# Replacing an implicit instruction schedule by one that is planned forward and backward: a bucketed attention, gated MLP and MLP kernel on one core

## The chip, the core and the metric

The kernel runs on one core of a Trainium2 chip. The core has five engines with a queue of instructions each: PE (matrix products and transposes), DVE (vector work), ACT (activations; it also issues some DMAs), POOL (elementwise work on GpSimd) and SP (it only issues DMAs here). Every engine takes its own queue strictly in order and waits where an operand isn't ready or a buffer isn't free. The metric is the time of one execution on the device in microseconds (us); of several executions the median is given.

## The reference

Three stages follow each other; B=2, H=8, S=768, D=64, model width 512. The reference in numpy, cut to what is computed:

```python
# attention: a key counts for a query only if both hash to the same bucket
q_bits = (einsum('bhsd,dk->bhsk', q, proj) > 0)        # 6 bits, likewise k_bits
mask = q_bucket[:, :, :, None] == k_bucket[:, :, None, :]
scores = where(mask, matmul(q, k.T) / sqrt(D), -1e9)
x = matmul(softmax(scores), v)                         # heads joined: (2, 768, 512)
# gated MLP with a product over the sequence
h = maximum(x @ w_in, 0); u, vh = h[..., :512], h[..., 512:]
v_n = (vh - mean(vh)) / sqrt(var(vh) + 1e-6)
v_s = einsum('ts,bsd->btd', w_spatial, v_n) + b_spatial[None, :, None]
y = (u * v_s) @ w_out
# second MLP with layernorm and residual
yn = (y - mean(y)) / sqrt(var(y) + 1e-6) * g_ln
return y + maximum(yn @ w_ch1, 0) @ w_ch2              # w_ch1 512x2048, w_ch2 2048x512
```

## The kernel before

Products are made in three passes of a 32-bit format: each operand is split into a high part (a rounded copy, on ACT or POOL) and a low part (the difference, on POOL or DVE), and high by high, high by low and low by high are added up. The three weights w_in, w_out and w1/w2 arrive as 64-bit floats. Each is taken in pieces of 512 columns (`stage_f64` loads one on ACT's queue into a tile `f64_...`, here written f_w, f_u, ...), turned into two 32-bit words on ACT and DVE (L102 to L107, tile f64c_...), added on POOL (L111) and split. w_out, w_v and w_u are converted during the attention, stored in device memory (`kept`) and loaded again for the second batch (`reload`, L515). The pieces of w1 and w2 are converted beside the second part and stay in SBUF.

Attention goes over 48 groups of two q tiles of 128 rows (batch, head, g). For one group PE makes the scores sc (L308, eight matmuls into the one PSUM buffer of that tag), DVE takes the maximum and clips (L319, tile x), ACT the exponential (L332), PE transposes x (pt, L346), ACT and DVE copy it to e, and PE multiplies with v (po, L360); ACT and DVE put the result into xT. Per pair of heads `pair_load` fetches k and q, `mismatch` makes the bucket signs (pm, m), `pair_split` the high and low parts (on POOL), and `passes_of` copies them by DMAs on SP's queue into ks and qs, from which sc is made. At the end of a pair `normalized` makes pz on PE and multiplies xT by it.

`moe1(b)` is the gated MLP of one batch, a generator that is advanced between other work: for six row tiles t, act_x (xT split), pv for the v half and later the u half, the statistics; then pg (product with w_spatial, pieces w_sp on SP's queue), gt (bias and gate, DVE L618), ptr_g (its transposes), act_g (its parts), py (product with w_out), y, and a store to y_dram. The first batch runs beside the attention of the second one. The second MLP works on three chunks c of 512 rows: layernorm of rows from y_dram (`ln_stats`: statistics bst_c, mv, scaling of xc; `ln_x`: px_c on PE, xh on ACT and DVE), then for each of 16 slices f `up` (pc, 12 matmuls, then ch on ACT and DVE) and `down` (12 matmuls into four tiles acc). Runs of (c, f) are c=0 and c=1 with f<5 first, then c=2 whole, then the rest of c=1 and c=0.

What sets the order before: the program is written in stages that are advanced by hand (`attn_step`, tables such as CONV_AT, `fill`), and Tile's own list scheduler, with a simulated time line (`schedule_with_timeline_sim=True`), reorders it. Parts of it are pinned: `tc.issue_after(...)` holds conversions, pair stages and w_sp loads behind the last maximum or exponential (CPIN, `last["late"]`), `mm3_after` chains the projections of batch 1, `high_priority` favours `moe1(1)`. The resulting order of every engine is fixed when the kernel is built.

Of the kernel before, what the change touches and what calls it, by code (L numbers as in the profile page):

```python
# [8 lines left out]
F32 = mybir.dt.float32  # L9
# [18 lines left out]

@with_exitstack
def attn_moe_kernel(ctx: ExitStack, tc: tile.TileContext, qT, kT, v, proj, w_in, w_spT, b_sp, w_out, g_ln, w1, w2, out):  # L30
    nc = tc.nc
# [20 lines left out]
    CPIN = ("max", "exp")  # L52
# [5 lines left out]
    PIN = (1,)  # L58
    HP = 0
# [197 lines left out]
    last = {}  # L257
# [55 lines left out]
    def masked_max(b, h, g, j):  # L313
# [5 lines left out]
        last["max"] = nc.vector.tensor_scalar(  # L319
# [121 lines left out]
    def mm3(ps, pairs):  # L441

        n, tot = 0, len(pairs) * 3
        for lh, rh in pairs:
            for i, j in PASSES:
                mm = nc.tensor.matmul(ps, lh(i), rh(j), start=(n == 0), stop=(n == tot - 1)).ins  # L446
                n += 1
        return mm

    def mm3_free(key, *args):  # L450
        mm3(*args)

    def mm3_after(key, *args):

        if key in last:
            with tc.issue_after(last[key]):
                last[key] = mm3(*args)
        else:
            last[key] = mm3(*args)
# [57 lines left out]
    def moe1(b, ps_m, tag):  # L517
# [19 lines left out]
        def v_half(t):  # L537
# [10 lines left out]
            last["moe"] = st_last[0]  # L548
# [57 lines left out]
        for t in range(NQT + 1):  # L606
            if t < NQT:
# [276 lines left out]
```

## Time and profile before

| | us |
|---|---|
| timed executions | 735.76, 735.81, 737.73 (median 735.81) |
| the profiled execution: its time | 737.73 |
| its span, first to last instruction | 737.7 |
| PE busy | 681.1 |
| DVE, ACT, POOL busy | 429.7, 310.8, 192.1 |
| mean granted PE clock | 0.971 of full |

The span starts with the first instruction and ends with the last; all positions below, such as 340–362, are us from its start. The attention of batch 0 runs to about 186; that of batch 1, with the gated MLP of batch 0 beside it, to about 350; the gated MLP of batch 1 with the first slices of the second MLP to about 475; the rest of the second MLP to the end.

### The profile page before, as it was taken

The numbers are of one execution on the slowest core, as the hardware profiler recorded it, in microseconds if no ns is written. First come the engines' busy times: TensorE is split into PE (matmuls) and PEld (weight loads), VectorE is DVE, ScalarE is ACT, GpSimd is POOL, SyncE is SP. The second block draws the span as 40 slices with busy tenths as digits, with TensorE's granted clock in tenths as the row PEclk, the third lists the DMA queues.
The fourth block names the chain that finished last, engine by engine and source line by source line (L and its number), as shares of the span: only waits on it lengthen the run. The fifth ranks groups of instructions, "written<-read, shape, count | busy, mean of one in ns | idle before, by whom it ended". The sixth has DMA issues, their size and how long they took to land.

```text
span 737.7 us, 10036 instructions
## 1 busy us (share of the span) xinstructions
PE 681.1 (92%) x3644; PEld 528.0 (72%) x3644; DVE 429.7 (58%) x818; ACT 310.8 (42%) x607; POOL 192.1 (26%) x189
## 2 busy tenths in 40 slices
PE   6998999895999999998899997799988899999997
PEld 5765667664777767776688886587766688888885
DVE  3586797784765645444898458676899812112112
ACT  2685878683565645444373231443232310100100
POOL 2224333315242222010143233234454500000000
PEclk8899999998999999999899998989999999999999
DMA  7664787575473563212533242533223101001001
GB/s 185 177 159 109 192 252 192 163 199 133 112 242 89 177 194 85 80 51 78 200 115 143 71 149 92 187 116 114 86 86 115 57 1 58 0 1 57 1 1 57
DMA packets 51514, 84.36 MB, mean 114 GB/s; under 512 B 6382, under 2 KB 35798, under 8 KB 50442
## 3 DMA queue, kind: packets, MB, share of 16 engines
q1 hardware_dynamic: 38426, 54.37, 26.1%
q10 hardware_dynamic: 13040, 29.36, 12.3%
q8 instruction: 29, 0.48, 0.3%
q14 instruction: 19, 0.16, 0.1%
HBM read 51.12 MB, written 12.58 MB: 86 GB/s over the span
## 4 chain that ended last, share of the span: by engine, by line
PE 60%; DMA 12%; DVE 12%; issue 5%; ACT 5%; POOL 4%; SPq 1%; ACTq 0%; DVEq 0%; POOLq 0%
PE acc L756 12%; PE pc L446 11%; PE pv L446 8%; PE sc L308 8%; PE po L360 6%; PE pg L616 5%; PE pt L346 5%; DMA f_w<-in_w 5%; PE py L446 3%; POOL f64c_w L111 2%; DMA wst_sp<-in_w_spT 2%; DVE f_w L105 2%; DVE x L319 1%; DMA f_u<-in_w_in 1%; ACT x L332 1%
## 5 line engine op out<-in xcount | busy, mean ns | idle before, releaser
L756 PE MATMUL acc<-w2t,ch 128*128 128x512 f32 x576 | 146.0, 396 | 7.7 <-DVE ch L747 6.3
L446 PE MATMUL pc<-xh,w1t 128*128 128x512 f32 x576 | 146.2, 399 | 2.7 <-DVE xh L740 2.7
L756 PEld LDWEIGHTS acc<-w2t,ch 128*128 128x128 f32 x576 | 106.9, 188 | 36.7 <-DVE ch L747 10.8
L446 PEld LDWEIGHTS pc<-xh,w1t 128*128 128x128 f32 x576 | 109.8, 191 | 28.5 <-ACT f64c_w L102 2.9
L319 DVE TENSOR_SCALAR_CACHE_REDUCE x<-sc 128x768 f32<-128x768 f32 x96 | 89.7, 951 | 32.3 <-PE sc L308 30.0
L308 PE MATMUL sc<-ks,qs 128*128 128x512 f32 (+3 forms) x384 | 86.4, 364 | 17.5 <-DMA ks<-k 8.3
L332 ACT ACTIVATE x<-x,nb 128x768 f32<-128x768 f32 x96 | 89.4, 933 | 26.3 <-DVE x L319 24.5
L747 DVE SCALAR_TENSOR_TENSOR ch<-pc,ch 128x512 fp32r<-128x512 f32 x48 | 33.0, 687 | 109.4 <-ACT ch L746 109.4
L346 PE MATMUL pt<-ident,x 128*128 128x128 f32 x576 | 81.2, 280 | 5.3 <-ACT x L332 3.0
L346 PEld LDWEIGHTS pt<-ident,x 128*128 128x128 f32 x576 | 67.9, 144 | 23.7 <-ACT x L332 9.5
L308 PEld LDWEIGHTS sc<-ks,qs 128*128 128x128 f32 (+1 forms) x384 | 59.2, 199 | 32.0 <-issue 21.1
L746 ACT ACTIVATE ch<-pc 128x512 fp32r<-128x512 f32 x48 | 28.4, 592 | 127.3 <-PE pc L446 127.3
L360 PE MATMUL po<-e,vv 128*64 128x256 f32 x576 | 75.0, 397 | 5.0 <-DVE m L247 1.9
L349 ACT ACTIVATE e<-pt 128x384 f32<-128x384 f32 x120 | 55.5, 487 | 34.5 <-PE pt L346 31.8
L111 POOL TENSOR_TENSOR f64c_w<-f_w,f64c_w 128x512 f32<-128x512 f32 x32 | 43.6, 1362 | 97.0 <-DVE f64c_w L107 82.9
L360 PEld LDWEIGHTS po<-e,vv 128*64 128x64 f32 x576 | 37.8, 139 | 29.8 <-issue 7.1
L351 DVE COPY e<-pt 128x384 f32<-128x384 f32 x72 | 39.6, 550 | 20.0 <-PE pt L346 19.7
L616 PE MATMUL pg<-vn,w_sp 128*128 128x512 f32 x180 | 46.8, 413 | 0.0
L102 ACT ACTIVATE f64c_w<-f_w 128x512 f32<-128x512 f32 x32 | 21.4, 670 | 58.3 <-DMA f_w<-in_w 51.1
L616 PEld LDWEIGHTS pg<-vn,w_sp 128*128 128x128 f32 x180 | 34.9, 198 | 8.0
L446 PE MATMUL pv<-w_u,act_x 128*128 128x512 f32 x144 | 37.9, 410 | 2.7 <-DMA w_u<-ws_u 2.7
L446 PE MATMUL py<-w_out,act_g 128*128 128x512 f32 x144 | 36.3, 396 | 2.1 <-ACT act_g L435 2.1
(133 smaller groups left out, 804.7 us busy)
## 6 DMA issues: line engine op xcount, KB each, us to landing
f_w<-in_w ACTq DMA_DIRECT2D x32, 512.0 KB
ks<-k SPq DMA_DIRECT2D x48, 192.0 KB
qs<-q SPq DMA_DIRECT2D x48, 128.0 KB
wst_sp<-in_w_spT SPq DMA_DIRECT2D x12, 384.0 KB
w_out<-ws_out SPq DMA_DIRECT2D x2, 2048.0 KB
vv<-in_v SPq DMA_DIRECT2D x16, 192.0 KB
qs<-q SPq DMA_DIRECT2D x48, 64.0 KB
ot<-y_dram SPq DMA_DIRECT2D x12, 256.0 KB
```

The source lines that it names most:

```text
L111: nc.gpsimd.tensor_tensor(cf, tf, cf, op=ALU.add)
L308: nc.tensor.matmul(sc[:, csl], qs[:rows, i, qsl], ks[:rows, i, csl], start=(i == 0), stop=(i == 1))
L319: last["max"] = nc.vector.tensor_scalar(x, t["sc"], MASKED, FMAX, op0=ALU.min, op1=ALU.min, accum_out=nb,).ins
L332: last["exp"] = nc.scalar.activation(t["x"], t["x"], AF.Exp, bias=t["nb"], scale=-1.0, accum_out=z_sum[b][:, n, h : h + 1]).ins
L346: nc.tensor.transpose(pt[:, i, :], t["x"][:, kt * P : (kt + 1) * P], ident)
L349: nc.scalar.activation(e, pt, AF.Copy)
L351: nc.vector.tensor_copy(e, pt)
L360: nc.tensor.matmul(po[a : a + D, :GW], heads[b, h]["vv"][:, kt], gr["e"][:, kt], start=(kt < 2), stop=(kt >= NKT - 2))
L446: mm = nc.tensor.matmul(ps, lh(i), rh(j), start=(n == 0), stop=(n == tot - 1)).ins
L616: nc.tensor.matmul(pg, w[i][:, k], vn[:, j, k, :], start=(n == 0), stop=(n == len(order3) - 1))
L747: last["lo"] = nc.vector.scalar_tensor_tensor(ch[:, 1], pc, 0.0, ch[:, 0].bitcast(F32), op0=ALU.max, op1=ALU.subtract).ins
L756: last["mm"] = nc.tensor.matmul(accs[c][t], ch[:, i, t * P : (t + 1) * P], w2t[f][:, j, 0, :], start=(start and n == 0), stop=(stop and n ...
```

## The change

The body of the kernel is hardly touched: the same calls `nc.tensor...`, `nc.vector...` are made in the same sequence, but `nc` is now a recorder (`Plan`). Tiles are placeholders (`Later`, `View`) and pools only notes (`Pool`, `Ring`). Every call becomes a `Job` with its engine, a cost from a small table (`cost`) and the jobs it must wait for; up to six matmuls of one shape into one tile are one job. `gates` adds the waits for free buffers. `run` goes forward through the jobs with one clock per engine: whichever engine can start first takes, of its jobs that are ready, the one with the smallest rank (by position in the program at first, later by the latest time at which it may start). Work of the other engines is opened only when PE has come within 60 jobs of it (LOOK) and not earlier than 20 us before it is due (EARLY). `latest` goes backward from the end and gives each job that due time. `settle` repeats the two twelve times and keeps the round with the earliest end. `issue` then emits all jobs by (part, start) under Tile's manual scheduling, so nothing reorders them any more. There are three parts: 0 is attention with `moe1(0)`, 1 `moe1(1)` with the first slices of the second MLP, 2 the rest; every engine finishes a part before it begins the next. All `issue_after`, `high_priority` and `mm3_after` are gone, and xc has eight buffers instead of six. No operation is added to or taken from the computation. In the trace of the changed kernel all instructions carry the line of `issue` (L476).

```diff
+    RUN = 6
+    LOOK = 60
+    EARLY = 20.0
+    ROUNDS = 12
...
+    def settle(self):
+        best = None
+        late = None
+        for n in range(self.ROUNDS):
+            end = self.run(late)
+            if best is None or end < best[0]:
+                best = (end, {j: (j.start, j.end) for j in self.jobs})
+            late = self.latest()
...
+            t, e, c = best
+            j = min((j for j in c if ready[j] <= t + 1e-9), key=rank)
...
+    def issue(self):
+        self.gates()
+        self.settle()
+        order = sorted((j for j in self.jobs if j.engine), key=lambda j: (j.part, j.start, j.at))
...
+        with self.tc.manual_schedule():
+            for j in order:
...
-    nc = tc.nc
+    fixed = ctx.enter_context(tc.tile_pool(name="fixed", bufs=1))
+    ident = fixed.tile([P, P], F32, name="ident")
+    make_identity(tc.nc, ident)
+    nc = plan = Plan(tc)
...
         for e in pair_steps.get(i, ()):
-            with tc.issue_after(last["exp"]):
-                e()
+            e()
...
-        xc = m2a.tile([P, DM], F32, tag="xc", name=f"xc_{c}_{len(xcs.setdefault(c, []))}", bufs=TPC + 2)
+        xc = m2a.tile([P, DM], F32, tag="xc", name=f"xc_{c}_{len(xcs.setdefault(c, []))}", bufs=TPC + 4)
...
+    plan.issue()
```

Three places of the new order. In the rows a name is followed by its batch, head or tile numbers and a running number; then come shape and count.

First, POOL at the start of batch 1 (k2_1_1 and q2_1_1 are the heads 2 and 3 of batch 1, act_x0 the parts of xT for `moe1(0)`; a TENSOR_SCALAR row is a high part, the 128x384 rows k's low part). Before:

```order
L228 TENSOR_SCALAR k2_1_1_1850<-k2_1_1_1850 128x768
L228 TENSOR_SCALAR q2_1_2_2293<-q2_1_2_2293 128x768
L86 TENSOR_TENSOR act_x0_0_2190<-xT_0_186,act_x0_0_2190 128x512
L86 TENSOR_TENSOR act_x0_1_2193<-xT_0_186,act_x0_1_2193 128x512
L86 TENSOR_TENSOR act_x0_2_2243<-xT_0_186,act_x0_2_2243 128x512
L86 TENSOR_TENSOR k2_1_1_1850<-k2_1_1_1850 128x384 x2
L111 TENSOR_TENSOR f64c_u_1_1816<-f64_u_1_1786,f64c_u_1_1816 128x512
L86 TENSOR_TENSOR w_u_0_1753<-f64c_u_1_1816,w_u_0_1753 128x512
```

and in the changed kernel:

```order
L476 TENSOR_SCALAR q2_1_1_1809<-q2_1_1_1809 128x768
L476 TENSOR_SCALAR k2_1_1_1816<-k2_1_1_1816 128x768
L476 TENSOR_TENSOR f64c_u_1_1811<-f64_u_1_1739,f64c_u_1_1811 128x512
L476 TENSOR_TENSOR k2_1_1_1816<-k2_1_1_1816 128x384 x2
L476 TENSOR_TENSOR w_u_0_1746<-f64c_u_1_1811,w_u_0_1746 128x512
L476 TENSOR_TENSOR act_x0_0_2071<-xT_0_347,act_x0_0_2071 128x512
L476 TENSOR_TENSOR act_x0_1_2121<-xT_0_347,act_x0_1_2121 128x512
L476 TENSOR_TENSOR act_x0_2_2133<-xT_0_347,act_x0_2_2133 128x512
```

The low part of k2_1_1 has moved from behind the three act_x0 to in front of them, and the high part of q2_1_2 no longer stands between k's high and low part.

Second, `moe1(1)` at its fifth row tile. On PE before, from the product pg_1_4 to the transposes ptr_g1_4 that need gt_1_4:

```order
L616 MATMUL pg_1_4_4583<-vn_1_3814,w_sp1_4_1_4478 128x512 x6
L616 MATMUL pg_1_4_4583<-vn_1_3814,w_sp1_4_0_4477 128x512 x11
L446 MATMUL py_1_3_4632<-w_out_1_4175,act_g1_3_4574 128x512
L616 MATMUL pg_1_4_4583<-vn_1_3814,w_sp1_4_0_4477 128x512
L446 MATMUL py_1_3_4632<-w_out_1_4175,act_g1_3_4574 128x512 x9
L446 MATMUL pc_0_4_4677<-xh_0_3964,w1t_4_4454 128x512
L446 MATMUL py_1_3_4632<-w_out_1_4175,act_g1_3_4574 128x512
L446 MATMUL pc_0_4_4677<-xh_0_3964,w1t_4_4454 128x512
L446 MATMUL py_1_3_4632<-w_out_1_4175,act_g1_3_4574 128x512
L433 MATMUL ptr_g1_4_4648<-ident_58,gt_1_4_4602 128x128 x4
L616 MATMUL pg_1_5_4656<-vn_1_3814,w_sp1_5_1_4580 128x512 x6
```

and in the changed kernel:

```order
L476 MATMUL pg_1_4_4550<-vn_1_3969,w_sp1_4_1_4493 128x512 x6
L476 MATMUL pg_1_4_4550<-vn_1_3969,w_sp1_4_0_4435 128x512 x12
L476 MATMUL acc_0_0_0_4283<-w2t_2_4447,ch_0_2_4405 128x512 x3
L476 MATMUL acc_0_0_1_4289<-w2t_2_4447,ch_0_2_4405 128x512 x3
L476 MATMUL acc_0_0_2_4296<-w2t_2_4447,ch_0_2_4405 128x512 x3
L476 MATMUL acc_0_0_3_4302<-w2t_2_4447,ch_0_2_4405 128x512 x3
L476 MATMUL py_1_3_4616<-w_out_1_4141,act_g1_3_4545 128x512 x12
L476 MATMUL ptr_g1_4_4634<-ident_58,gt_1_4_4593 128x128 x4
L476 MATMUL pc_0_4_4642<-xh_0_4023,w1t_4_4527 128x512 x6
```

Between the end of pg_1_4 and ptr_g1_4 there now stand the twelve acc matmuls and the whole of py_1_3. On DVE, which makes gt_1_4, the rows in front of it were

```order
L167 BN_AGGR mv_1_4531<-bst_c1_1_4539 128x2
L105 SCALAR_TENSOR_TENSOR f64_w1_5_4894<-f64_w1_5_4894,f64c_w1_5_4896 128x512
L83 TENSOR_TENSOR w_sp1_5_1_4580<-wst_sp1_5_4577,w_sp1_5_0_4579 128x768
L167 BN_AGGR mv_1_4531<-bst_c1_2_4544 128x2
L724 SCALAR_TENSOR_TENSOR xc_1_0_4532<-xc_1_0_4532,mv_1_4531,g_bc_3801 128x512
L166 BN_STATS bst_c2_0_4803<-xc_2_0_4528 128x6
L167 BN_AGGR mv_1_4531<-bst_c1_3_4549 128x2
L724 SCALAR_TENSOR_TENSOR xc_1_1_4537<-xc_1_1_4537,mv_1_4531,g_bc_3801 128x512
L106 TENSOR_SCALAR f64c_w1_5_4896<-f64_w1_5_4894 128x512
L724 SCALAR_TENSOR_TENSOR xc_1_2_4542<-xc_1_2_4542,mv_1_4531,g_bc_3801 128x512
L103 TENSOR_SCALAR f64c_w2_5_4909<-f64c_w2_5_4909 128x512
L618 SCALAR_TENSOR_TENSOR gt_1_4_4602<-pg_1_4_4583,b_sb_94,xT_1_1709 128x512
```

and are now

```order
L476 SCALAR_TENSOR_TENSOR f64c_w2_3_4481<-f64_w2_3_4438,f64c_w2_3_4481 128x512
L476 BN_STATS bst_c1_0_4560<-xc_1_0_4466 128x6
L476 TENSOR_TENSOR w_sp1_5_1_4569<-wst_sp1_5_4496,w_sp1_5_0_4547 128x768
L476 BN_AGGR mv_1_4571<-bst_c1_0_4560 128x2
L476 BN_STATS bst_c1_1_4575<-xc_1_1_4472 128x6
L476 SCALAR_TENSOR_TENSOR ch_0_3_4557<-pc_0_3_4458,ch_0_3_4557 128x512
L476 BN_AGGR mv_1_4571<-bst_c1_1_4575 128x2
L476 BN_STATS bst_c1_2_4588<-xc_1_2_4484 128x6
L476 SCALAR_TENSOR_TENSOR gt_1_4_4593<-pg_1_4_4550,b_sb_2768,xT_1_1915 128x512
```

Two scalings of xc_1, statistics of chunk 2 and conversion steps that stood before gt_1_4 stand behind it; a ch stands before it now.

Third, PE where attention ends and `moe1(1)` begins (py_0_5 the last product of batch 0, pv_1_t_1 the v half and pv_1_t_0 the u half of tile t, w_u_1 the weight loaded anew). Before:

```order
L433 MATMUL ptr_g0_5_3740<-ident_58,gt_0_5_3687 128x128 x4
L446 MATMUL py_0_5_3748<-w_out_0_2789,act_g0_5_3745 128x512 x2
L360 MATMUL po_1_7_2_3764<-e_1_7_2_3689,vv_1_7_3390 64x256 x6
L385 MATMUL pz_1_3_0_3779<-ident_58,zw_1_3_0_3777 128x128 x3
L385 MATMUL pz_1_3_1_3786<-ident_58,zw_1_3_1_3784 128x128 x3
L446 MATMUL py_0_5_3748<-w_out_0_2789,act_g0_5_3745 128x512 x10
L446 MATMUL pv_1_0_1_3823<-w_v_1_3000,act_x1_0_3815 128x512 x12
L446 MATMUL pv_1_1_1_3856<-w_v_1_3000,act_x1_1_3819 128x512 x12
L446 MATMUL pv_1_0_0_3915<-w_u_1_3803,act_x1_0_3815 128x512 x12
L446 MATMUL pv_1_2_1_3946<-w_v_1_3000,act_x1_2_3852 128x512 x12
```

and in the changed kernel:

```order
L476 MATMUL py_0_4_3713<-w_out_0_2889,act_g0_4_3679 128x512 x6
L476 MATMUL pt_1_7_2_1_0_3723<-ident_58,x_1_7_2_1_3662 128x128 x3
L476 MATMUL pt_1_7_2_1_1_3724<-ident_58,x_1_7_2_1_3662 128x128 x3
L476 MATMUL po_1_7_1_3725<-e_1_7_1_3631,vv_1_7_3452 64x256 x6
L476 MATMUL py_0_5_3757<-w_out_0_2889,act_g0_5_3737 128x512 x12
L476 MATMUL po_1_7_2_3773<-e_1_7_2_3720,vv_1_7_3452 64x256 x6
L476 MATMUL pz_1_3_0_3783<-ident_58,zw_1_3_0_3693 128x128 x3
L476 MATMUL pz_1_3_1_3787<-ident_58,zw_1_3_1_3701 128x128 x3
L476 MATMUL pv_1_0_1_3833<-w_v_1_3569,act_x1_0_3817 128x512 x12
L476 MATMUL pv_1_1_1_3851<-w_v_1_3569,act_x1_1_3821 128x512 x12
L476 MATMUL pv_1_2_1_3875<-w_v_1_3569,act_x1_2_3826 128x512 x12
L476 MATMUL pv_1_0_0_3874<-w_u_1_3815,act_x1_0_3817 128x512 x12
```

ptr_g0_5 stands directly ahead of the first row shown of the new order. py_0_5 now stands before po_1_7_2 and pz instead of around them, and three v halves stand before the first u half instead of two. At the very end of PE's queue the twelve matmuls that finish c=0 were ordered as two for each of the four acc and then one for each; now each acc gets its three in one piece.

## Rows read from the trace of the kernel before

**Rows 1.** The page, part 1: busy us (share of the span) and instructions
```profile
PE 681.1 (92%) x3644; PEld 528.0 (72%) x3644; DVE 429.7 (58%) x818; ACT 310.8 (42%) x607; POOL 192.1 (26%) x189
```

**Rows 2.** By stretch: its length, busy us (instructions) per engine, PEclk, DMA share, GB/s
```profile
24.00:148.00 124.00, 112.67 (x826) 80.26 (x824) 96.69 (x203) 92.70 (x203) 42.29 (x40) 0.99 0.65 177
148.00:186.00 38.00, 28.49 (x203) 20.51 (x202) 24.46 (x56) 22.35 (x49) 13.32 (x13) 0.91 0.62 162
186.00:340.00 154.00, 151.88 (x926) 117.62 (x927) 86.48 (x187) 80.61 (x163) 37.70 (x33) 1.00 0.42 122
340.00:362.00 22.00, 17.24 (x85) 12.21 (x84) 12.54 (x23) 7.49 (x13) 0.00 (x0) 0.90 0.64 219
...
446.00:480.00 34.00, 24.77 (x104) 19.43 (x103) 26.09 (x54) 11.17 (x19) 10.23 (x7) 0.86 0.40 137
480.00:590.00 110.00, 102.27 (x429) 79.28 (x428) 89.78 (x129) 37.61 (x63) 51.20 (x39) 0.98 0.30 94
```

**Rows 3.** What PE waited for: us in total, times, longest us
```profile
PE sc L308 <- DMA ks<-k: 8.3, 1, 8.3
PE acc L756 <- DVE ch L747: 6.3, 8, 1.6
PE ptr_g L433 <- DVE gt L618: 4.3, 1, 4.3
...
PE sc L308 <- DMA qs<-q: 3.2, 1, 3.2
...
PE pv L446 <- DMA w_u<-ws_u: 2.7, 1, 2.7
```

**Rows 4.** The chain that ended last, 160 to 184: start us, us, what
```profile
166.03 4.63 DMA qs<-m
...
171.25 3.70 POOL act_x L86 x3
174.96 1.91 POOL k L86 x2
...
176.89 2.59 DMA ks<-k
```

**Rows 5.** PE in order of time, 165 to 186: start us, us, what [idle before]
```profile
167.72 1.69 PE L308 MATMUL sc<-ks,qs 128*128 128x512 f32 x8 [0.28 <-DVE x L319]
169.25 0.82 PE L346 MATMUL pt<-ident,x 128*128 128x128 f32 x6
...
179.83 2.90 PE L308 MATMUL sc<-ks,qs 128*128 128x512 f32 x8 [8.32 <-DMA ks<-k]
```

**Rows 6.** PE in order of time, 345 to 366
```profile
353.16 5.66 PE L446 MATMUL pv<-w_v,act_x 128*128 128x512 f32 x24
```

**Rows 7.** The chain that ended last, 350 to 364
```profile
353.36 8.02 DMA w_u<-ws_u
```

**Rows 8.** The chain that ended last, 430 to 450 and 515 to 560
```profile
436.45 7.73 DMA f_w<-in_w
...
525.71 3.62 DMA f_w<-in_w
```

**Rows 9.** By stretch, for the tile f64c_w alone: busy us (instructions)
```profile
488.00:590.00 102.00, 70.93 (x90) 23.51 (x37) 47.51 (x37) 1.00 0.30 91
```

**Rows 10.** The tile f_w, 488 to 590: ns min/median/max, first and last start
```profile
L105 DVE SCALAR_TENSOR_TENSOR f_w<-f_w,f64c_w x18: 683/1384/1811, 493.2 to 585.1; 128x512 uint32<-128x512 uint32 x18
```

**Rows 11.** All engines in order of time, 726 to 738
```profile
726.88 5.60 PE L756 MATMUL acc<-w2t,ch 128*128 128x512 f32 x24
...
731.84 2.48 DVE L766 TENSOR_TENSOR ot<-acc,ot 128x512 f32<-128x512 f32 x4 [3.44 <-PE acc L756]
```

**Rows 12.** DVE groups, 24 to 148: count | busy us, mean ns | idle before, releaser
```profile
L319 DVE TENSOR_SCALAR_CACHE_REDUCE x<-sc 128x768 f32<-128x768 f32 x47 | 43.9, 949 | 11.6 <-PE sc L308 9.5 <-ACT w_sp L80 1.9
L351 DVE COPY e<-pt 128x384 f32<-128x384 f32 x23 | 12.7, 550 | 2.4 <-PE pt L346 2.2
```

More of the change, by code (lines that the diff above doesn't have):

```diff
@@ new lines, with __init__, allocated, allocate @@
+class Later(View):
+    def __init__(self, ring, shape, dtype, name):
+        self.shape, self.ring, self.name, self.tile = shape, ring, name, None
+        self.at, self.uses, self.gate = len(ring.tiles), [], None
+        super().__init__(self, (), tuple((0, n) for n in shape), tuple(range(len(shape))), dtype)
+        ring.tiles.append(self)
+    def allocated(self):
+        self.ring.allocate(self.at)
+        return self.tile
+class Ring:
+    def __init__(self, pool, tag, bufs):
+        self.pool, self.tag, self.bufs, self.tiles, self.done = pool, tag, bufs, [], 0
+    def allocate(self, at):
+        while self.done <= at:
+            t = self.tiles[self.done]
+            t.tile = self.pool.real.tile(t.shape, t.dtype, tag=self.tag, name=t.name, bufs=self.bufs)
+            self.done += 1
@@ new lines, with __init__, tile, psum @@
+class Pool:
+    def __init__(self, plan, name, bufs=1, part=0, after=(), **how):
+        self.plan, self.name, self.bufs, self.part, self.after, self.how = plan, name, bufs, part, after, how
+        self.rings, self.real, self.gate = {}, None, None
+        plan.pools.append(self)
+    def tile(self, shape, dtype, tag=None, name=None, bufs=None):
+        tag = tag or name
+        if tag not in self.rings:
+            self.rings[tag] = Ring(self, tag, bufs or self.bufs)
+        return Later(self.rings[tag], shape, dtype, name)
+    @property
+    def psum(self):
+        return self.how.get("space") == PSUM
+    def users(self):
+        return {j for r in self.rings.values() for t in r.tiles for j, _, _ in t.uses}
@@ new lines, with __init__, __getattr__, cells @@
+class Job:
+    def __init__(self, at, engine, part):
+        self.at, self.engine, self.part = at, engine, part
+        self.calls, self.after, self.busy, self.lag, self.bytes = [], set(), 0.0, 0.0, 0
+        self.start = self.end = None
+        self.shared = False
+class Engine:
+    def __init__(self, plan, key):
+        self.plan, self.key = plan, key
+    def __getattr__(self, op):
+        return lambda *args, **kw: self.plan.add(self.key, op, args, kw)
+def cells(x):
+    if isinstance(x, View):
+        return x.columns
+    n = 1
+    for d in x.shape[1:]:
+        n *= d
+    return n
@@ L445, in mm3 @@
             for i, j in PASSES:
-                mm = nc.tensor.matmul(ps, lh(i), rh(j), start=(n == 0), stop=(n == tot - 1)).ins
+                nc.tensor.matmul(ps, lh(i), rh(j), start=(n == 0), stop=(n == tot - 1))
                 n += 1
[L448 to L459, printed above, removed]
     w_split = {}
@@ L687, in attn_moe_kernel @@
         pass
-    del last["late"]
-    att.close()
+    plan.part = 1
     NA = 5
@@ L755, in down @@
             for n, (i, j) in enumerate(PASSES):
-                last["mm"] = nc.tensor.matmul(
+                nc.tensor.matmul(
                     accs[c][t],
@@ L819, in attn_moe_kernel @@
     for n in range(24):
-        with tc.high_priority(offset=HP):
-            next(m1, None)
+        next(m1, None)
         for e in fill.get(n, ()):
-            with tc.issue_after(last["moe"]):
-                e()
+            e()
     for _ in m1:
         pass
-    moe.close()
-    m2 = ctx.enter_context(tc.tile_pool(name="m2", bufs=1, side="right", reuse_waits="tile"))
+    plan.part = 2
+    m2 = Pool(plan, "m2", 1, part=2, after=(mp,), side="right", reuse_waits="tile")
     for t in range(TPC):
```

389 lines of the change are left out of this document (344 added, 45 removed).

## The prediction

> **What bounds the kernel now.** I first read the page's busy lines [rows 1]: PE works 681.1 of 737.7 us, so 56.6 us of idle PE time are all that another order can win, apart from what a lowered clock costs. Next the busy time by stretches [rows 2], cut where the page's slices changed. From 186 to 340 PE is all but full (2.1 us idle). Idle time sits in five others: 11.3 us in the attention part (24–148), 9.5 in 148–186, 4.8 in 340–362, 9.2 in 446–480, 7.7 in 480–590. In three of them the granted clock is low as well: 0.91, 0.90 and 0.86. Last the list of PE's waits [rows 3], which says what ended the idle time: one wait of 8.3 us for a copy of ks, one of 4.3 for gt, eight on ch (6.3 together), one of 2.7 for w_u. DVE, the next busiest engine, has 58% [rows 1]. So PE bounds the kernel, with holes made by what stood in front of the awaited step on other engines.
>
> **The change part by part.** No arithmetic and no size goes (only xc gets two more buffers); the five engines' streams are put in another order. So each term is a hole of before, against what the new order has at that place.
>
> First, ks (148–186). The chain of waits [rows 4] shows POOL making the low part of act_x three times (3.70 us) before the low part of k (1.91), then the copy of ks (2.59), then PE. In the new order k's low part stands ahead of all three act_x. That takes 3.70 us out of the chain, and POOL no longer stands before it waiting for the copy of qs that frees the next pair's q (4.63 us [rows 4]). Together that is 8.33, so I count the whole wait of 8.3 [rows 3]; bounds 3.7 and 8.3. After the wait PE ran slow: eight score matmuls took 2.90 us, where eight took 1.69 before it [rows 5]. Over the stretch the granted clock is 0.91, against 0.99 in 24–148; on 28.49 busy us [rows 2] that is 2.3, and I take 2. Term: -10.3.
>
> Second, attention (24–148). Its 11.3 idle us are many small waits. Bounds 0 and 11.3; the nearest row is 186–340, the same loop with more matmuls to fill with, where 2.1 is left [rows 2]. With less to fill with I take a third: -4.
>
> Third, the seam 340–362. Of its 4.8 idle us, 2.7 are the wait for w_u [rows 3]; the other 2.1 lie before py_0_5, for act_g. Now half of py_0_4, six transposes and a po stand between ptr_g0_5 and py_0_5, some 2.5 us, which hides act_g. Three groups of v (36 matmuls, at 5.66 us for 24 [rows 6] 8.5 us) stand ahead of the first group of u, where two stood. The load of w_u (8.02 us [rows 7]) still goes out when py_0_5 is done; behind py_0_5 come po and pz (2.3 us at full clock), a new hole, and those 8.5, so it is covered. The new hole is this: py_0_5 used to lie between pz and the first pv. Now nothing does, while xs, act_x high and act_x low are made, three steps over 512 columns or fewer, at the 0.68 us of the shortest L105 [rows 10] at most 2 us. Won 4.8, lost 2: -3, with the clock's share (0.90) as margin.
>
> The loads there are a risk. The first pieces f_w (0.5 MB each on ACT's queue, 3.62 us undisturbed [rows 8]) now go out together with w_u (2 MB on SP's), where before the first of them had gone out long ago. If they don't disturb each other, the term stands. The Trainium skill ("DMA: Bandwidth & Descriptors", Issuing engines are not separate DMA queues) says that transfers from different issuing engines end on the same 16 DMA engines and interleave. The trace agrees: an f_w beside other loads took 7.73 us [rows 8]. By that rule three pieces and w_u take up to 8.0 + 10.9 = 18.9 us against some 12.8 of cover, and the third term would be +3 instead of -3.
>
> Fourth, 446–480. Before, DVE had statistics and scalings of the second MLP's layernorm, a w_sp low part and conversion steps in front of gt_1_4, and PE waited 4.3 [rows 3]. Now two statistics and one ch stand directly in front of it, and 24 matmuls (acc and py, 5.66 us) stand between pg_1_4 and the transposes of gt: -4.3. The other 4.9 of the 9.2 lie around px_c1 and px_c2, before the first pc of the next rows. Now acc matmuls (c=0, f=4) lie between those px_c, and px_c2 is spread among the pc: -4. The clock, 0.86 against 0.99 on 24.77 busy us [rows 2], costs 3.2; I take 2.7. Term: -11.
>
> Fifth, 480–590. PE waits for ch because DVE's queue has conversion steps in front of it, some of them long: L105 took between 0.68 and 1.81 us [rows 10]. Before, more than one weight piece is converted per step of PE (24 matmuls, 5.66 us [rows 6]), and all are finished four steps before the last is used; now it is one piece a step, from before ch_1_0 to the end of c=2. With less DVE work a step I take 5 of 7.7, bounds 0 and 7.7. Term: -5.
>
> Sixth, the end. The last matmuls end at 726.88 + 5.60 = 732.48; as they went over the four acc in turn, the four adds ran from 731.84 to 734.32 [rows 11], 1.84 us past them. Now each acc is finished by its own three matmuls, and only the last add (0.62) remains behind: -1.2.
>
> Seventh, the start. All 36 warm-up transposes now stand ahead of pm, where 30 did, and proj is loaded third. Six transposes take 0.82 us [rows 5]; the wait for qs before the first scores is 3.2 [rows 3]. I take +0.7; bounds 0 and 2.
>
> Sum: -10.3 - 4 - 3 - 11 - 5 - 1.2 + 0.7 = -33.8. New holes that the order alone doesn't show will appear; two of the size of w_u's [rows 3] are +5.4. So -28.4, and 737.7 - 28.4 = 709.3 in the profiled execution. That is the slowest of the three that were timed (737.73, equal to its span) and 1.9 above their median; against the median I predict 707.
>
> **The rivals.** (a) Only the two long waits go, with clock (10.3, and 4.3 + 2); the seams and conversions give back what they take: 737.7 - 16.6 - 1.9 = 719. For it speak the loads at the seam, and that one piece a step leaves conversion no reserve. A piece holds one of two f64 buffers for its load (3.62 [rows 8]), half of ACT's 1.31 us a piece, DVE's 3.94 and half of POOL's 2.64 (23.51, 70.93 and 47.51 over 18 pieces [rows 9]): 9.5, so a piece every 4.8 us; with a load of 7.73 every 6.8, over PE's 5.66. Against it: the step's other work on DVE is one ch.
>
> A rule bears on the conversions. The Trainium skill ("SBUF — State Buffer", Who interferes with whom) has DVE operations with two SBUF inputs and GpSimd operations block each other wholly. The spread of L105 [rows 10] agrees. If all of DVE's 3.94 had to stand apart from POOL's 2.64, a piece would take 6.6 us and case (a) would hold; the 3.94 contains such blocking already, so I give it no more.
>
> (b) Nearly all goes. Left are the start (7 us), the end (4), 4 in attention and 4 elsewhere, 19 of the 56.6 [rows 1]; the clock gives 6: 737.7 - 37.6 - 6 - 1.9 = 692. For it: 186–340 shows that PE can be kept full [rows 2]. Against it: attention has little to fill with.
>
> (c) It doesn't do what it says: both streams are fixed per engine, and the waits only move: 736.
>
> (d) Slower. One score buffer serves 48 groups of q tiles: a group's scores can't start until DVE has taken both maxes of the group before (0.95 us each [rows 12]), and PE covers that with pt and po. Where the new order of DVE puts an e copy (0.55 [rows 12]) or more ahead of the second max, 0.55 to 0.95 us are exposed in each group. It decides once DVE's work between two groups of scores exceeds PE's; in 24–148 DVE has 96.7 to PE's 112.7 [rows 2], 14% to spare. At 0.75 us in 48 groups it is 36: 707 + 36 = 743. Against it: PE's new order keeps transposes between the scores.
>
> **How the numbers follow.** Forecast 0.60, with its own range 697 to 718; (a) 0.17, (b) 0.11, (c) 0.04, (d) 0.08. The range takes in the forecast, (a) and most of (b): 690 to 729, with about 0.15 outside. What a measurement of this kernel can tell from no change is 0.3%, 2.2 us. Faster are the forecast, (a) and (b), less a little at the edge of (a): 0.87; same is (c), 0.04; slower (d) and that edge, 0.09.
>
> **What would show it.** In the profile after: no wait of PE for ks over 1 us, and the granted clock near 0.99 where it was 0.91; no wait for gt; the first group of u without a wait for w_u, but about 2 us for act_x behind pz; waits for ch under 2 us in total; one add behind the last matmul. PE's busy time should fall by about 6 us (clock) and its idle time by some 23. I am wrong if a wait for w_u, w1t or w2t of over 5 us appears, if sc waits for x in most groups, or if attention keeps its 11 idle us.

## The result and the profile after

The changed kernel takes 692.29 us (four executions, 691.43 to 693.03) against 735.78: ratio 0.941, 95% interval 0.9388 to 0.9432, so 43.5 us or 5.9% faster. That lies inside the predicted range (690 to 729), 15 us under the forecast of 707 and on the figure of rival (b), 692. The profiled execution took 692.87 (span 691.1) and is compared below with that of before (span 737.7): 46.6 us apart. One execution of a later run (proj first; 2413.8 us, where its other three took 691.8 to 696.1) is a slow one and left out of that run's time.

The page's busy line after, in the form of [rows 1]:

```profile
PE 666.3 (96%) x3644; PEld 521.2 (75%) x3644; DVE 446.1 (65%) x818; ACT 310.5 (45%) x607; POOL 194.8 (28%) x189
```

PE's idle time fell from 56.6 to 24.8 us (691.1 - 666.3), by 31.8; its busy time fell by 14.8 for the same 3644 matmuls. The forecast had 23 and 6.

What PE still waits for, as in [rows 3] (us in total, times, longest); the groups behind these come to 1.4 us or less each:

```profile
PE pv L476 <- ACT xT L476: 3.8, 2, 2.0
PE acc L476 <- DVE ch L476: 2.2, 1, 2.2
PE sc L476 <- issue: 2.0, 1, 2.0
PE sc L476 <- DMA qs<-q: 1.9, 1, 1.9
PE sc L476 <- DVE x L476: 1.7, 3, 1.3
PE pv L476 <- DVE act_x L476: 1.6, 2, 1.3
```

Neither ks nor gt nor w_u is left. To see where the time went, both traces are cut at the same pieces of work: first scores; first scores of batch 1; scores of its fifth head; last pz; first pc of chunk 2; last matmul. The scores of batch 1 begin at 141.01 before, so the stretch 148–186 [rows 2], with the wait for ks, lies in batch 1; that batch 0's attention runs to about 186, as the overview has it, is wrong. Before (length, busy us and count per engine, granted clock, DMA share, GB/s):

```profile
12.89:141.01 128.12, 114.97 (x815) 82.87 (x815) 95.75 (x200) 91.67 (x200) 40.68 (x38) 0.95 0.64 169
141.01:229.38 88.37, 78.50 (x514) 58.52 (x513) 59.83 (x134) 54.14 (x115) 32.30 (x31) 0.96 0.61 172
229.38:350.62 121.24, 117.24 (x708) 90.09 (x707) 60.04 (x124) 58.09 (x116) 21.16 (x19) 0.99 0.38 110
350.62:507.79 157.17, 145.25 (x637) 117.64 (x637) 114.01 (x230) 62.09 (x107) 51.58 (x39) 0.95 0.39 132
507.79:732.48 224.69, 216.96 (x925) 172.22 (x923) 92.95 (x124) 40.95 (x68) 41.20 (x32) 1.00 0.13 43
```

and after:

```profile
10.78:127.42 116.64, 110.47 (x815) 81.36 (x815) 97.92 (x205) 92.26 (x201) 40.53 (x38) 0.97 0.65 167
127.42:204.69 77.27, 76.10 (x522) 57.25 (x520) 59.08 (x126) 51.80 (x110) 31.10 (x29) 1.00 0.57 152
204.69:322.08 117.39, 117.39 (x715) 90.08 (x713) 59.87 (x127) 57.57 (x117) 25.01 (x22) 1.00 0.48 148
322.08:469.31 147.23, 140.45 (x628) 112.88 (x627) 118.81 (x216) 61.96 (x105) 43.95 (x34) 0.97 0.44 148
469.31:686.83 217.52, 214.46 (x925) 173.00 (x923) 106.17 (x141) 43.88 (x73) 49.71 (x37) 1.00 0.16 52
```

The gains are 11.5, 11.1, 3.9, 9.9 and 7.2 us; with 2.1 before the first scores (12.89 to 10.78) and 1.0 behind the last matmul they make 46.6 (before rounding). In the first row PE does 815 matmuls in both: it idles 13.2 us before and 6.2 after, and is busy 4.5 us less. The third row has no idle time at all now.

Part of this is the clock. In the stretches where half of the full clock was granted (1.2 of 2.4 GHz), the trace of before shows (seven stretches; the first, the last and the sum)

```profile
12.90:23.10 10.20, 8.22 (x29) 6.83 (x30) 3.92 (x8) 3.75 (x8) 0.00 (x0) 0.50 0.63 157
...
477.10:483.90 6.80, 5.51 (x13) 4.23 (x14) 6.80 (x18) 1.00 (x2) 1.41 (x1) 0.50 0.77 266
sum 40.90, PE 32.96 PEld 25.23 DVE 23.62 ACT 12.65 POOL 10.64; mean PE 4.71 PEld 3.60 DVE 3.37 ACT 1.81 POOL 1.52
```

and that of after, two in all:

```profile
13.00:19.90 6.90, 5.45 (x21) 4.73 (x21) 3.46 (x9) 3.08 (x7) 0.00 (x0) 0.51 0.76 184
340.70:350.90 10.20, 7.24 (x20) 5.54 (x21) 8.17 (x21) 6.37 (x12) 1.60 (x1) 0.50 0.00 0
sum 17.10, PE 12.69 PEld 10.27 DVE 11.64 ACT 9.45 POOL 1.60; mean PE 6.35 PEld 5.13 DVE 5.82 ACT 4.73 POOL 0.80
```

At half clock a busy us does half a us of work: 33.0 busy us cost 16.5 before, 12.7 cost 6.3 after. So about 10 of the 46.6 us are, by this estimate, clock that was lost behind holes and no longer is. (The same matmuls timed at both levels in the rows of the first scores below differ by 1.7 to 1.9, 2.90 to 1.69 and 2.76 to 1.48; by that it is 8.5 to 9.4.) The rest of the 14.8 us by which the busy time fell, some 5 to 6 us, isn't explained; 2.5 of it lie in the last row, where both clocks are full. (Both traces have a further stretch behind the last matmul, where it costs nothing.)

### The profile page after: what moved, and what is told of

It is laid out like the page before. It is cut to its first block, busy times and chain, and to the rows that moved or that the text cites. A ratio compares the mean times of both kernels' runs of the same rounds, so it can differ in the third digit from the quotient of the medians.

```text
span 691.1 us, 10094 instructions
## 1 busy us (share of the span) xinstructions
PE 666.3 (96%) x3644; PEld 521.2 (75%) x3644; DVE 446.1 (65%) x818; ACT 310.5 (45%) x607; POOL 194.8 (28%) x189
## 3 DMA queue, kind: packets, MB, share of 16 engines
q10 hardware_dynamic: 13040, 29.36, 13.2%
## 4 chain that ended last, share of the span: by engine, by line
PE 64%; DMA 13%; DVE 12%; issue 3%; ACT 3%; POOL 3%; SPq 1%; ACTq 0%; POOLq 0%; DVEq 0%
PE acc L476 10%; PE pc L476 10%; PE pv L476 8%; PE sc L476 8%; PE pt L476 7%; PE po L476 7%; PE pg L476 7%; DMA f_w<-in_w 6%; DVE f64c_w L476 6%; PE py L476 4%; POOL f64c_w L476 2%; DVE f_w L476 2%; DMA f_v<-in_w_in 2%; SPq L476 1%; DMA ks<-k 1%
## 5 line engine op out<-in xcount | busy, mean ns | idle before, releaser
L476 PE MATMUL pc<-xh,w1t 128*128 128x512 f32 x576 | 142.9, 395 | 0.9 <-POOL w1t L476 0.6
L476 PE MATMUL acc<-w2t,ch 128*128 128x512 f32 x576 | 141.6, 393 | 2.2 <-DVE ch L476 2.2
L476 PEld LDWEIGHTS acc<-w2t,ch 128*128 128x128 f32 x576 | 107.8, 188 | 26.8 <-DVE ch L476 2.6
L476 PEld LDWEIGHTS pc<-xh,w1t 128*128 128x128 f32 x576 | 107.5, 188 | 26.5 <-POOL w1t L476 1.4
L476 ACT ACTIVATE x<-x,nb 128x768 f32<-128x768 f32 x96 | 89.3, 931 | 29.9 <-DVE x L476 29.8
L476 DVE SCALAR_TENSOR_TENSOR ch<-pc,ch 128x512 fp32r<-128x512 f32 x48 | 33.0, 687 | 99.9 <-ACT ch L476 99.9
L476 DVE TENSOR_SCALAR_CACHE_REDUCE x<-sc 128x768 f32<-128x768 f32 x96 | 88.4, 951 | 13.4 <-PE sc L476 12.2
L476 PE MATMUL sc<-ks,qs 128*128 128x512 f32 (+3 forms) x384 | 88.2, 360 | 5.8 <-issue 2.0
L476 PE MATMUL pt<-ident,x 128*128 128x128 f32 x576 | 81.5, 277 | 2.2 <-ACT x L476 1.2
L476 PEld LDWEIGHTS pt<-ident,x 128*128 128x128 f32 x576 | 68.0, 142 | 19.2 <-issue 5.6
L476 ACT ACTIVATE ch<-pc 128x512 fp32r<-128x512 f32 x48 | 28.5, 593 | 113.5 <-PE pc L476 111.2
L476 POOL TENSOR_TENSOR f64c_w<-f_w,f64c_w 128x512 f32<-128x512 f32 x32 | 43.7, 1366 | 109.1 <-DVE f64c_w L476 106.6
L476 PE MATMUL po<-e,vv 128*64 128x256 f32 x576 | 72.8, 388 | 1.2 <-ACT e L476 1.2
L476 ACT ACTIVATE e<-pt 128x384 f32<-128x384 f32 x120 | 55.6, 489 | 33.7 <-PE pt L476 31.3
L476 PEld LDWEIGHTS sc<-ks,qs 128*128 128x128 f32 (+1 forms) x384 | 57.8, 193 | 16.7 <-DVE x L476 4.6
L476 DVE COPY e<-pt 128x384 f32<-128x384 f32 x72 | 39.7, 553 | 31.8 <-PE pt L476 31.4
L476 PEld LDWEIGHTS po<-e,vv 128*64 128x64 f32 x576 | 37.0, 136 | 26.2 <-issue 5.4
L476 DVE TENSOR_SCALAR f64c_w<-f64c_w 128x512 f32<-128x512 f32 (+1 forms) x64 | 42.7, 667 | 16.1 <-ACT f64c_w L476 15.0
L476 ACT ACTIVATE f64c_w<-f_w 128x512 f32<-128x512 f32 x32 | 21.5, 671 | 56.4 <-DMA f_w<-in_w 56.4
L476 PE MATMUL pg<-vn,w_sp 128*128 128x512 f32 x180 | 45.3, 400 | 0.4 <-ACT y L476 0.4
L476 PE MATMUL pv<-w_v,act_x 128*128 128x512 f32 x144 | 38.0, 411 | 4.4 <-ACT xT L476 1.8
L476 PEld LDWEIGHTS pg<-vn,w_sp 128*128 128x128 f32 x180 | 32.9, 188 | 8.5 <-ACT y L476 0.8
```

Source lines behind the costliest of these rows:

```text
L476: getattr(getattr(nc, engine[j.engine]), op)(*map(live, args), **{k: live(x) for k, x in kw.items()})
```

## The experiments

All times are medians of several executions, and every kernel is compared with runs of the kernel before on the same chip; these had medians of 735.2 to 736.8, so the ratios are the safer measure. In the kernels whose finished order was edited, `issue` stands at L516.

**Due times.** The planner with its forward pass alone, `ROUNDS = 1`, and then with one backward pass, `ROUNDS = 2`.

> The changed kernel with one round of planning instead of twelve: the forward pass alone, jobs ranked by their place in the program, no due times from a backward pass. Theory D (due times carry the gain): the order falls back towards the program's, 705 to 735 us. Rival F (a forward pass with durations that fit the chip is enough, and the rounds only polish): 692 to 700 us.

732.0 us, ratio 0.9951 (0.9924 to 0.9977): nearly all of the gain is gone, theory D. By the same cuts (third and last row left out):

```profile
13.19:145.57 132.38, 114.52 (x815) 83.25 (x815) 99.29 (x205) 94.12 (x201) 39.75 (x38) 0.94 0.64 175
145.57:232.86 87.29, 78.86 (x519) 58.77 (x519) 61.05 (x127) 52.66 (x112) 30.83 (x28) 0.98 0.52 134
...
348.03:504.87 156.84, 145.60 (x640) 115.96 (x638) 124.06 (x217) 63.05 (x106) 46.57 (x34) 0.97 0.43 143
```

The attention of batch 0 is worse than before (17.9 us idle, 0.94 granted clock) although every duration the pass uses is the same as in the changed kernel. This run has the changed kernel's recorder, its manual scheduling and its eight xc buffers, so none of these brings the gain by itself.

> The changed kernel with two rounds of planning: one forward pass by program order, one backward pass, one forward pass by due times (the better of the two is kept). With one round the time was 732.0. Theory D1 (the due times of a single backward pass carry the gain): 692 to 702 us. Rival D2 (the passes have to be repeated, each on the schedule of the one before): 706 to 725 us.

696.2 us, ratio 0.9468 (0.9431 to 0.9506), theory D1: one backward pass brings 36 of the 40 us between 732 and 692, the ten further rounds the rest.

**The place of k's low part on POOL, from both sides.** In the finished order of the changed kernel its two instructions were put behind act_x0_0; the other engines' orders are unchanged:

```diff
  POOL
- k2_1_1 128x384 x2
  w_u_0
  act_x0_0
+ k2_1_1 128x384 x2
  act_x0_1
```

> The changed kernel with one edit of its finished order: on POOL the low part of k2_1_1 stands behind act_x0_0 instead of three places ahead of it, so by the trace of the changed kernel it starts at about 156.8 us instead of 148.3, 8.5 us later; every other engine keeps its order. Theory A (POOL's place for k's low part made the long wait of the kernel before): PE waits for ks again, 3 to 8 us, and 1 to 2 us of slow clock follow, 696 to 702 us. Rival B (the new order has so much slack around this copy that the place no longer matters, and the gain came from elsewhere): no wait for ks over 1 us, 691 to 694 us.

699.7 us, ratio 0.9519 (0.9467 to 0.9571) against 0.941: 8 us slower, theory A. PE in order of time (the view calls the wait "issue"; it stands before the first scores of head 2, which need that ks, and ks's copy is issued at 156.66, when POOL has made the low part):

```profile
159.43 1.19 PE L516 MATMUL sc<-ks,qs 128*128 128x512 f32 x2 [4.72 <-issue]
160.43 1.48 PE L516 MATMUL pt<-ident,x 128*128 128x128 f32 x6
```

A hole of 4.7 us, and transposes that take 1.48 us for six instead of 0.82 [rows 5] behind it.

The other way, in the kernel before, by holding instructions behind k's low part. Here Tile's scheduler orders everything anew, and instructions of the other engines move as well (in the second run some 20 on PE, 30 on ACT and 25 on DVE), so these two runs change more than POOL's order:

```diff
+                if b == 0 and t < 3:
+                    with tc.issue_after(last["klo", 1, 1]):
+                        split_lo(hl[:, 1], src, hl[:, 0])
...
+                    if (b, r, nm) == (1, 2, "q"):
+                        pins.enter_context(tc.issue_after(last["klo", 1, 1]))
```

First the act_x alone (the first three lines, there with `last["klo"]`, which is the same low part by POOL's order):

> The kernel before with only the three low parts of act_x0 held behind the low part of k2_1_1 on POOL; the high part of q2_1_2, which waits for a copy of qs, still stands in front of it. Theory A (the chain of waits read literally): 3.7 us of the 8.3 go, the wait for ks is about 4.6 us and the time about 731 to 732 us. Rival B: the whole wait goes, about 726 us. Rival C (waits only move): 735 to 737 us.

734.0 us, ratio 0.9974 (0.9941 to 1.0006): not told apart from no change. In the profile the wait before the scores of head 2 is 3.6 us now, ended by the copy of m into ks,

```profile
PE sc L308 <- DMA ks<-m: 3.6, 1, 3.6
```

so 4.7 of the 8.3 went, more than the 3.7 of theory A, and the stretch from the first scores of batch 1 to those of head 2 is 34.2 us instead of 38.8. But up to the fifth head only 1.9 us of these 4.6 are left: behind the wait 6.9 us run at half clock (180.0 to 186.9) where 3.8 did before, and PE waits 0.9 us for ACT. Then both edits:

> The kernel before with the low part of k2_1_1 ahead of the high part of q2_1_2 and of the three low parts of act_x0 on POOL. Theory A (first term of the prediction, -10.3 us): the wait of 8.3 us for ks goes, and with it about 2 us of slow clock, 724 to 727 us. Rival B (something else is late directly behind it): a new wait of 3 us or more within the next 10 us, 730 to 733 us. Rival C (nothing): 735 to 737 us.

728.4 us, ratio 0.9883 (0.9848 to 0.9919): 8.6 us faster by the ratio, 7.8 by the medians. The interval takes in the forecast of -10.3, but the median misses the 724 to 727 of theory A. No wait for ks is left, and batch 1 up to the fifth head takes 80.6 us instead of 88.4, at full clock:

```profile
140.62:221.22 80.60, 76.60 (x514) 57.10 (x513) 61.03 (x134) 54.67 (x115) 35.06 (x31) 1.00 0.66 189
```

So this one place is worth about 8 us, of the 11.1 in that stretch: shown cleanly in the changed kernel, where only POOL's order was edited, and in the kernel before with the reordering named above.

**The first loads.** proj ahead of k_raw and q_raw on SP again:

> The changed kernel with the load of proj moved back to the front of SP's queue, ahead of k_raw and q_raw, as before. Theory L (the order of the first loads is what brought the first scores from 12.89 forward to 10.78 us): the first scores start at 11.7 to 12.9 us and the time rises by 1 to 3 us, to 693 to 695 us. Rival M (the casts of m and the issue of qs on SP set the start): the first scores stay within 0.4 us of 10.78 and the time within 0.5 us.

The first scores start at 11.88, as theory L says, and now run slowly, since PE waits longer before them:

```profile
11.88 2.70 PE L516 MATMUL sc<-ks,qs 128*128 128x512 f32 x8 [3.40 <-DMA qs<-q]
```

The time is 693.5 us (three executions), and its ratio of 0.9433 (0.9395 to 0.9470) overlaps the changed kernel's. About half of the 2.1 us at the start is shown; its effect on the whole isn't.

**A filler against the slow clock.** In the changed kernel the second group of scores waits for the only score buffer and then runs slowly:

```profile
10.78 1.69 PE L476 MATMUL sc<-ks,qs 128*128 128x512 f32 x8 [1.88 <-DMA qs<-q]
14.45 2.90 PE L476 MATMUL sc<-ks,qs 128*128 128x512 f32 x8 [1.98 <-issue]
17.14 2.76 PE L476 MATMUL pt<-ident,x 128*128 128x128 f32 x12
```

```diff
+            warm3 = ps_b.tile([P, P], F32, tag="b", name="warm3")
+            for _ in range(18):
+                nc.tensor.transpose(warm3, ident, ident)
```

> The changed kernel with 18 transposes of the identity, read by nobody, on PE between the first and the second group of scores, where PE waits 1.98 us for the one score buffer. Theory C (the wait lowers the granted clock and the slow matmuls behind it cost time): the second group of scores takes about 1.7 us instead of 2.90 and the twelve transposes behind it 1.5 instead of 2.76, and the time falls by 1.5 to 2.5 us. Rival N (DVE and ACT set the pace there, so faster matmuls only wait): the same durations fall, but the time stays within 0.5 us.

```profile
12.46 2.13 PE L516 MATMUL warm<-ident 128*128 128x128 f32 x18
14.61 1.66 PE L516 MATMUL sc<-ks,qs 128*128 128x512 f32 x8
16.10 1.48 PE L516 MATMUL pt<-ident,x 128*128 128x128 f32 x12
```

The durations fall as both theories say. 691.1 us, ratio 0.9401 (0.9370 to 0.9431), can't be told from 0.941. The profile reaches batch 1 2.1 us earlier, but so does the run with k behind act_x (125.3 in both against 127.4), which has the same order up to there and no filler: that much attention varies between executions. Open.

**The seam at 322 to 351.** This is the largest hole left. The trace of the changed kernel: the first weight piece is loaded beside w_u, in the chain of waits

```profile
322.66 9.93 DMA f_w<-in_w
```

ACT in order of time (ACTq is a DMA issue in its queue)

```profile
322.66 0.39 ACTq L476 DMA_DIRECT2D f_w<-in_w  x1
...
333.36 0.60 ACT L476 ACTIVATE vr<-pv 128x512 f32<-128x512 f32 x1
337.54 0.39 ACTq L476 DMA_DIRECT2D f_w<-in_w  x1
337.97 0.63 ACT L476 ACTIVATE w1t<-f64c_w 128x512 fp32r<-128x512 f32 x1 [4.01 <-POOL f64c_w L476]
338.51 0.61 ACT L476 ACTIVATE act_x<-xT 128x512 fp32r<-128x512 f32 x1
339.03 0.58 ACT L476 ACTIVATE xT<-pv 128x512 f32<-128x512 f32 x1
```

and PE

```profile
332.22 5.60 PE L476 MATMUL pv<-w_u,act_x 128*128 128x512 f32 x24
339.66 0.73 PE L476 MATMUL pv<-w_v,act_x 128*128 128x512 f32 x2 [1.83 <-ACT xT L476]
341.69 2.07 PE L476 MATMUL pv<-w_v,act_x 128*128 128x512 f32 x4 [1.30 <-DVE act_x L476]
345.73 2.93 PE L476 MATMUL pv<-w_u,act_x 128*128 128x512 f32 x6 [1.97 <-ACT xT L476]
```

ACT stands between 333.96 and 337.54 although act_x and xT behind it are wanted. First one instruction was moved, the high part of w1t_0 behind xT:

> The changed kernel with one instruction moved on ACT: the high part of w1t_0, which waits for a weight piece whose load took 9.93 us there, stands behind act_x1_3 and the first xT of the u half instead of ahead of them. Theory S (the late load stands in ACT's queue in front of what PE needs): the waits of 1.83 and 1.30 us of the seam go, 688 to 690 us. Rival T (DVE's conversion steps and statistics are what is late; ACT's place doesn't matter): 691 to 693 us, with the same 5 us of waits.

691.2 us, ratio 0.9400 (0.9363 to 0.9438), with 1.20, 1.80 and 2.69 us of waits, 5.7 together: theory S fails in this form, and time and waits are those of rival T. ACT shows that its queue stood still all the same:

```profile
335.55 0.39 ACTq L516 DMA_DIRECT2D f_w<-in_w  x1
336.03 0.63 ACT L516 ACTIVATE act_x<-xT 128x512 fp32r<-128x512 f32 x1 [4.06 <-PE pv L516]
336.57 0.58 ACT L516 ACTIVATE xT<-pv 128x512 f32<-128x512 f32 x1
```

The issue of the next load (335.55) was still in front; it waits until one of the two f64 buffers is free, and so for the late piece. Then four moves:

```diff
  ACT
- load f64_w1_1
- w1t_0 high
  act_x1_3 high
  xT <- pv_1_0_0
+ xT <- pv_1_1_0
+ load f64_w1_1
+ w1t_0 high
  ...
- xT <- pv_1_1_0
  DVE
  f64c_w1_0 (last step)
+ act_x1_3 low
  ... (13 rows)
- act_x1_3 low
```

> The changed kernel with four instructions moved in the finished order at the seam, PE's order untouched. On ACT the second xT of the u half comes directly behind the first, and the load of the weight piece w1_1 (a DMA issue that waits for a free f64 buffer) and the high part of w1t_0 come behind both instead of in front; on DVE the low part of act_x1_3 comes ahead of four statistics. Theory Q (in the run with one move on ACT the queue still stood behind the DMA issue that waits for its buffer, so that the late weight piece blocked ACT all the same): PE's waits of 1.8, 1.3 and 2.0 us there fall below 1.5 in total, the 10.2 us of slow clock behind them go, and the time is 682 to 688 us. Rival R (PE's own order and the three act buffers make the hole): the waits stay above 3 us and the time within 1.5 us of 692.

The three waits are gone, and one longer one is there, for the layernorm of xc:

```profile
337.18 1.52 PE L516 MATMUL pv<-w_v,act_x 128*128 128x512 f32 x6
338.54 1.52 PE L516 MATMUL pv<-w_u,act_x 128*128 128x512 f32 x6
345.22 1.97 PE L516 MATMUL px_c<-ident,xc 128*128 128x128 f32 x8 [5.16 <-ACT xc L516]
```

690.6 us, ratio 0.9388 (0.9355 to 0.9421). What blocked ACT is as theory Q says: ahead of act_x1_3 it was idle for 4.06 us there, and is for 1.26 now. As DVE's order was changed in the same run, what each of the two engines had in the three waits isn't separated, so rival T isn't ruled out for its part. The time of theory Q isn't reached, since xc is just as late: its statistics stand behind the conversion on DVE and begin at 336.07, against 336.03 in the changed kernel. With px_c moved back on PE and the filler:

> The changed kernel with the four moves on ACT and DVE of the run before, and two more on PE: px_c0_0 and px_c0_1, on which PE then waited 5.2 us, come behind the twelve pv matmuls that need nothing more, and 18 transposes of the identity, read by nobody, fill the 2.0 us between the first two groups of scores. Theory Q2 (what is left at the seam is the late layernorm of xc, and 2.8 us of matmuls in front cover as much of it): the wait for xc falls from 5.2 to about 2.4, both stretches of slow clock (6.8 us each) shrink or go, and the time is 683 to 688 us. Rival R2 (each move only uncovers the next late step, and the seam takes what it takes): the wait turns up elsewhere and the time is 689 to 692 us.

690.7 us, ratio 0.9382 (0.9346 to 0.9417): the wait for xc falls to 2.6, and two for xh appear, 2.4 together. The first stretch of slow clock is gone, the one at the seam (344.6 to 351.5) is not. Rival R2. None of these versions is shown to be faster than the changed kernel.

**The planner's transfer model.** It took a transfer for delayed by at most its own length.

```diff
-both = max(0.0, min(queue[other] - begin, 2 * span)) / 2
+both = max(0.0, min(queue[other] - begin, 8 * span)) / 2
```

> The changed kernel planned anew with one number of its transfer model changed: a transfer beside a longer one of the other queue is delayed by up to four times its own length instead of once. Theory S (the plan took the first weight pieces at the seam for landed 6 us too early and put ACT's and DVE's work behind them): the waits at the seam (5 us for xT and act_x) shrink below 2.5, and the time is 686 to 690 us. Rival P (a new plan is no better, it only moves its holes): 691 to 695 us.

695.2 us, ratio 0.9458 (0.9431 to 0.9486). By the same cuts, from the first scores of batch 1 on:

```profile
128.04:216.17 88.13, 84.83 (x556) 63.79 (x555) 63.63 (x132) 55.02 (x116) 31.08 (x30) 0.98 0.53 146
216.17:327.98 111.81, 111.21 (x676) 85.55 (x675) 58.78 (x124) 54.86 (x111) 24.19 (x21) 1.00 0.45 145
327.98:469.73 141.75, 137.59 (x627) 110.50 (x626) 114.52 (x211) 59.98 (x103) 42.14 (x32) 1.00 0.45 152
469.73:689.69 219.96, 215.48 (x925) 172.65 (x923) 110.05 (x146) 45.12 (x75) 51.22 (x39) 1.00 0.16 52
```

The stretch of the seam (from 327.98) is 5.5 us shorter than after the change and its clock is full: theory S for the seam. But the two ahead of it are 5.3 longer together (the cut between them falls elsewhere in this order) and the last is 2.4 longer: rival P for the whole. Restricted to parts 1 and 2 (`8 if j.part else 2`):

> The changed kernel planned anew with the altered transfer model for parts 1 and 2 alone; part 0 keeps the old one, though its order changes too since due times run backward through all parts. In the run with the altered model everywhere the stretch from the last pz to the first scores of chunk 2 was 5.5 us shorter, and the attention of batch 1 5.3 us longer. Theory S (the model belongs to the seam): the seam keeps its 5 us and the time is 684 to 689 us. Rival P (each new plan reshuffles attention, and its holes vary by as much as the seam gives): 690 to 697 us.

693.3 us, ratio 0.9424 (0.9389 to 0.9458): rival P again. The fourth stretch takes 146.9 us here, so even at the seam the gain of the other plan wasn't the model's alone.

## Why the prediction was right, and where its sizes were off

Direction and range were right, and so was the mechanism: no work went, PE's holes did. The forecast's own range, 697 to 718, was missed. Of the 18.2 us between the forecast saving of 28.4 and the 46.6 of the profiles, 7.5 are the attention, 5.4 the allowance for new holes, 2.8 the start and 2.2 the conversions; the other terms differ by less than 1 each. Step by step, in the profiled execution:

- ks, -10.3: the stretch gave 11.1, and the two-sided experiment puts about 8 of it on the place that the order rows showed. The step holds. The chain's 3.70 us of act_x alone took 4.7 off the wait, but only 1.9 of that lasted to the fifth head, and the time isn't told apart from no change.
- Attention, -4: 11.5. This is the step that failed most. I took a third of its 11.3 idle us because there is little to fill with. The waits there were not for lack of work: with the same 815 matmuls 7.0 us of idle time went. Of the 13.2 us before, some 9 ended on a step of ACT or DVE; which engine's order mattered was not tested. The forward-only run (17.9 us idle) shows that this hangs on the due times. I also cut the attention stretch at 24 us [rows 2] and so left out the 10.2 us of half clock before it, of which 6.9 are left.
- The seam and 446 to 480, -3 and -11: 9.9 plus the 3.9 of the stretch before, 13.8 for 14. The waits for w_u, gt, mv and xh are gone. But the sum is right by two errors: the seam, forecast -3, idles more than before (PE's five waits from 323 to 346 come to 6.4 us, against 4.8 in [rows 2]), and what lies behind it gained more. The risk was named and came true in another form: f_w took 9.93 us beside w_u, yet w_u was in time and what stood still was ACT's queue. The Trainium skill ("DMA: Bandwidth & Descriptors", Issuing engines are not separate DMA queues) has such transfers share the same DMA engines. The 9.93 us agree with it, but the price fell on another engine than I had it.
- Conversions, -5: 7.2, of which 4.7 are idle time (7.7 to 3.1) and 2.5 the unexplained busy time. PE waits 2.2 and 0.3 us for ch, a little more than the 2 in total that I had named, and 0.6 for w1t. One piece a step left enough reserve, so rival (a) didn't come about.
- The end, -1.2: 1.0. One add remains behind the last matmul, as forecast; it takes 0.69 us, not 0.62:

```profile
681.23 5.60 PE L476 MATMUL acc<-w2t,ch 128*128 128x512 f32 x24
...
684.83 2.73 DVE L476 TENSOR_TENSOR ot<-acc,ot 128x512 f32<-128x512 f32 x4 [2.08 <-PE acc L476]
```

The matmuls end at 686.83; the four adds follow each other without a gap, the last from 686.87 to 687.56, 0.73 us past the matmuls instead of 1.84 [rows 11].

- The start, +0.7: -2.1. I counted the warm-up transposes, which lie beside the loads, and not k_raw's load, which comes one place earlier; moving proj back costs 1.1 of it. Where the other half comes from is open.
- The +5.4 for holes that the order doesn't show: no such loss appears on top of the terms. The seam's new waits are inside its own term.
- The clock: I took 4.7 us; the stretches at half clock gave about 10 by the estimate above.

Rival (d) shows nowhere: the waits of sc for x are 1.7 us in all. What rival (b) was given, 0.11, was too little: the evidence for it, a stretch of 154 us with PE full [rows 2], was in the rows. That its 692 fits so closely is luck, though: it left 19 us of idle time and gave the clock 6, while the profile has 24.8 us idle and 14.8 us less busy time.

## What to carry to other kernels

Where many short holes of the bounding engine have different causes, price them as one question, whether the order is bad or the work is missing. A stretch of the same loop that is already full is a sign that it is the order, as it was here. A hole that lowers the clock costs, besides its own length, about half the busy time of the slow matmuls behind it (by the estimate above 16.5 of 33.0 us before), so read the granted clock with the idle time. And in this planner the due times from one backward pass were worth 36 us, the ten further rounds 4, and a changed figure for transfers nothing.

## What the runs showed of the hardware

- A 0.5 MB load that took 3.62 us undisturbed took 9.93 us beside a load of 2 MB and six of 0.25 to 0.4 MB from the other queue.
- A DMA issue in ACT's queue that waits for a buffer holds back the activations behind it; no row names this wait, one sees only ACT idle before the next activation (4.06 us in the run with one move, 1.26 with the issue put behind them).
- After waits of 1.9 to 2.0 us PE's clock was halved in some places (the second scores, 2.90 us for eight matmuls) and not in others (the first scores, 1.69, after 1.88 us). After 3.2 and 3.4 us the first scores ran slowly too (2.89 before, 2.70 with proj first).
- Of the 32 steps of L105 on f_w before, ten took 1.30 to 1.81 us, and each of these ran beside a POOL instruction for 0.75 to 1.27 us; the others took 0.65 to 0.70 us, with at most 0.39 us of POOL beside them.
- Four kernels with the same order up to batch 1 reach it between 125.3 and 127.7 us, so single profiles don't settle 2 us there.
